# A linear-attention and two-MLP kernel: scores in column tiles of 32 keys, and column-tiled work in sessions

## The chip, the cores and the metric

One core of one Trainium2 chip. The metric is the time of one execution on the device, in microseconds (us); lower is better. A core has five engines: TensorE (PE; the profile has its weight loads as PEld), VectorE (DVE), ScalarE (ACT), GpSimd (POOL) and SyncE (SP), which here issues most of the DMAs. PE writes its results to PSUM, which has eight banks of 128 partitions by 512 floats; all other tiles lie in SBUF.

## The reference, cut to what matters

Three stages. A gated linear attention with a complex decay for 4 sequences of 768 steps, 8 heads of 48; a gated MLP without a nonlinearity; and a second MLP with 8 experts, of which each token takes one.

```python
for t in range(S):
    new_re = ar * S_re - ai * S_im
    new_im = ar * S_im + ai * S_re
    kv = np.einsum('bhd,bhe->bhde', k[:, :, t], v[:, :, t])
    S_re, S_im = (new_re + kv, new_im)
    y[:, :, t] = np.einsum('bhd,bhde->bhe', q[:, :, t], S_re)
x = y.transpose(0, 2, 1, 3).reshape(3072, 384)
x = (x @ w_a) * (x @ w_b) @ w_out
e = argmax(x @ w_gate);  out = gate * (relu(x @ w1[e]) @ w2[e])
```

## The kernel before, in words

**Blocks and chunks.** The 3072 tokens are cut into 12 blocks of 256 (`j` = 0 to 11; the text calls `j` = 3 the fourth), three blocks to a sequence, and each block into two chunks `c` of 128. The recurrence is worked out chunk by chunk in matrix form: within a chunk, scores of 128 keys by 128 queries under a causal mask; between chunks, a state `T`.

**Preprocessing** (`pre`, from L1139). From a, q and k it works out decays and phases on ACT, DVE and POOL, in tiles of which there is one each. Its last operations are the products of L1275 (k and q with the cosine and the sine, on POOL for most blocks) and twelve DMAs on SP (L1286, the turning loads) that set these products into `kT` and `qT`: 96 rows (real and imaginary part of 48) by head, chunk and token. The next block's preprocessing reuses the tiles that these DMAs read, and the next block's `kT` and `qT` those of this block.

**Attention** (`attn`, L1317 to 1443), for each chunk:

- `sc` (L1332 to 1335): scores, 4 heads to a PSUM bank, one product for each head over all of PE's 128 columns. An f32 product is two passes of PE, so four heads are eight passes.
- `mask` (L1337): DVE reads the bank, multiplies by the causal mask (-1 or 0) and writes `sm`.
- `kn` and `kept` (L1341, L1346): PE transposes `kT`, four heads at a time, and ACT copies the result to SBUF.
- `y` (L1351 to 1374): the output, in column tiles of 32: four products stand side by side on PE's 32-column strips. Each adds `sm` times v and `qT` times the state.
- `kv` (L1390 to 1394): the state's update, in three column tiles of 32; `sum_` and `fade` (L1396, L1405) apply it on DVE.
- `xH`, `xL` (L1381, L1387): y in two parts, which the MLP reads.

v of a chunk (L1109) lies in one of three buffers, with 64 floats to a head, of which 48 are loaded.

**The first MLP** (`planned_moe`, L1074), one block later: for each of 12 slices of the hidden width, `up` (18 products of 256 columns, L957), a gate on ACT, DVE and POOL (L974 to 991), and `down` (6 products of 392 columns, L1000). Block j - 1's MLP runs beside block j's attention and block j + 1's preprocessing.

**The order.** Every engine executes its instructions in the order in which the program lists them. Up to the last block's MLP that order comes from a planner (`Plan`, from L343). Each operation is given to it with an engine, a duration, what it reads and writes, and a due time `at`; it plays through the schedule and lets each engine take, of what is ready, the operation that is due first. `TIMES` (L47) shifts the due times of kinds of operations; the kinds numbered 4 are all blocks from the fifth on. Due times of successive blocks lie `SLOT` = 48.9 apart. The score banks are a ring of three (`P = Plan({"sc": 3})`, L834): scores, transposes, `kv` and the router's count take them in turn. Loads on SP wait in its queue, in the planner's order, until their buffer is free.

**The start.** POOL writes constants (L482 to 505, L1102) before its first preprocessing product (L1201).

**The end.** After the plan the last block's MLP and the experts run in an order of their own (from L1513).

## Time and profile before

| | us |
|---|---|
| median of 3 runs | 912.55 |
| lowest, highest run | 911.75, 915.97 |
| the profiled execution, its own time | 914.04 |
| its span, first to last instruction | 912.2 |
| mean granted TensorE clock in it | 0.992 |

The profile is of one execution. A span is the time from the first to the last instruction; the execution's own time has a little more around it. A product's duration in the timeline runs from its start to its modelled end, and products overlap; so the cost of a product on PE is read from the start of one to the start of the next. `x8` in a row counts the passes merged into it. "Idle before" is the time that the engine stood still ahead of an instruction, with what ended it in brackets.

### The profile page before, as it was taken

Reading aid. Unit: us, or ns where it says so; the run is one execution under the profiler, and the core shown is the slowest. Engines: PE = TensorE matmul, PEld = TensorE weight load, DVE = VectorE, ACT = ScalarE, POOL = GpSimd, SP = SyncE. Lnnn points to the kernel's source line nnn. Section 1 sums busy time; section 2 is a strip of 40 time slices with the busy share of each in tenths; the row PEclk is TensorE's granted clock in tenths of the full one; section 3 lists DMA queues with packets and bytes.
Section 4 is the critical chain, followed back from the end, with each engine's and each line's share of the span. In section 5 each row is a group of like instructions: output and inputs, shape, how many; then the busy total and the mean of one; then the engine's idle time right before and its main releaser. Section 6 shows DMA issues by size and latency. Waiting matters only on the chain.

```text
span 912.2 us, 20675 instructions
## 1 busy us (share of the span) xinstructions
PE 850.9 (93%) x8188; PEld 816.7 (90%) x8188; DVE 557.2 (61%) x1217; ACT 477.2 (52%) x887; POOL 352.5 (39%) x338
## 2 busy tenths in 40 slices
PE   0399999999999999999999999999995999999995
PEld 0387899999999999999999999999995999999995
DVE  6999997683838475666757593445731545455540
ACT  6487887574656474655655552224521534344430
POOL 2341441414454545363544444204163343444311
PEclk9999999999999999999999999999997999999998
DMA  9999964433242452627274524123341544454511
GB/s 254 276 279 236 244 142 124 103 90 100 69 96 81 109 170 65 200 60 217 63 208 69 167 59 145 36 88 122 105 153 35 160 133 138 147 161 129 164 51 25
DMA packets 134379, 120.17 MB, mean 132 GB/s; under 512 B 37284, under 2 KB 128820, under 8 KB 134271
## 3 DMA queue, kind: packets, MB, share of 16 engines
q1 hardware_dynamic: 121151, 100.51, 39.3%
q0 software_dynamic: 11392, 17.43, 8.3%
q8 instruction: 67, 1.10, 0.5%
q10 hardware_dynamic: 1728, 0.79, 0.4%
q14 instruction: 41, 0.34, 0.2%
HBM read 82.42 MB, written 10.56 MB: 102 GB/s over the span
## 4 chain that ended last, share of the span: by engine, by line
PE 72%; issue 13%; DMA 5%; POOL 5%; DVE 3%; SPq 1%; ACT 0%; POOLq 0%; DVEq 0%; ACTq 0%
PE ab_p L957 31%; PE o L1000 16%; PE h_p L771 4%; PE sc_p L1335 4%; PE y_p L1374 4%; PE o L803 4%; PE ab_p L965 3%; POOL gt L732 2%; POOL out_dram L814 2%; PE o L971 2%; PE kv_p L1394 2%; DMA out_dram<-ye,ids 1%; PE kn_p L1344 1%; DMA v<-in_v_dram 1%; DMA ids<-idtab 1%
## 5 line engine op out<-in xcount | busy, mean ns | idle before, releaser
L957 PE MATMUL ab_p<-xH,wL 128*128 128x256 f32 x792 | 220.9, 279 | 0.0
L957 PEld LDWEIGHTS ab_p<-xH,wL 128*128 128x128 f32 x792 | 148.8, 188 | 0.0
L991 POOL TENSOR_TENSOR gL<-g,gH 128x256 fp32r<-128x256 f32 x96 | 80.3, 838 | 171.4 <-ACT gH L987 166.9
L980 ACT COPY g<-ab_p 128x256 f32<-128x256 f32 x132 | 48.8, 370 | 133.6 <-PE ab_p L957 124.3
L983 DVE TENSOR_TENSOR g<-g,ab_p 128x256 f32<-128x256 f32 (+1 forms) x148 | 60.7, 410 | 90.3 <-ACT g L980 87.0
L957 PE MATMUL ab_p<-xH,waH 128*128 128x256 f32 x396 | 113.7, 287 | 0.0
L957 PE MATMUL ab_p<-xL,waH 128*128 128x256 f32 x396 | 111.1, 281 | 0.0
L957 PE MATMUL ab_p<-xH,wbH 128*128 128x256 f32 x396 | 110.6, 279 | 0.0
L957 PE MATMUL ab_p<-xL,wbH 128*128 128x256 f32 x396 | 110.4, 279 | 0.0
L1000 PE MATMUL o<-woH,gH 128*128 128x392 f32 x264 | 96.4, 365 | 0.0
L1000 PE MATMUL o<-wL,gH 128*128 128x392 f32 x264 | 90.3, 342 | 0.0
L1000 PE MATMUL o<-woH,gL 128*128 128x392 f32 x264 | 90.2, 342 | 0.0
L771 PE MATMUL h_p<-sH,w1H 128*128 128x256 f32 (+5 forms) x240 | 78.2, 326 | 11.2 <-issue 10.2
L803 PE MATMUL o<-w2H,h 128*128 128x384 f32 (+3 forms) x312 | 86.2, 340 | 0.0
L771 PE MATMUL h_p<-sL,w1H 128*128 128x256 f32 (+5 forms) x240 | 77.4, 323 | 0.0
L771 PE MATMUL h_p<-sH,w1L 128*128 128x256 f32 (+5 forms) x240 | 77.4, 322 | 0.0
L987 ACT ACTIVATE gH<-g 128x256 fp32r<-128x256 f32 x132 | 54.5, 413 | 40.3 <-DVE g L983 36.7
L957 PEld LDWEIGHTS ab_p<-xH,waH 128*128 128x128 f32 x396 | 74.5, 188 | 0.9 <-issue 0.2
L957 PEld LDWEIGHTS ab_p<-xL,waH 128*128 128x128 f32 x396 | 74.6, 188 | 0.4
L957 PEld LDWEIGHTS ab_p<-xL,wbH 128*128 128x128 f32 x396 | 74.5, 188 | 0.0
L957 PEld LDWEIGHTS ab_p<-xH,wbH 128*128 128x128 f32 x396 | 74.4, 188 | 0.0
L814 POOL DMA_INDIRECT out_dram<-ye,ids x29 | 30.2, 1040 | 92.9 <-ACT ye L813 84.2
(210 smaller groups left out, 2162.8 us busy)
## 6 DMA issues: line engine op xcount, KB each, us to landing
raw<-in_moe_w_dram SPq DMA_DIRECT2D x64, 384.0 KB
q<-in_q_dram SPq DMA_DIRECT2D x24, 192.0 KB
v<-in_v_dram SPq DMA_DIRECT2D x24, 192.0 KB
raw<-in_moe_w_a_dram SPq DMA_DIRECT2D x12, 384.0 KB
raw<-in_moe_w_b_dram SPq DMA_DIRECT2D x12, 384.0 KB
raw<-in_moe_w_out_dram SPq DMA_DIRECT2D x12, 384.0 KB
wL<-a POOLq DMA_DIRECT2D x24, 192.0 KB
x2d<-x SPq DMA_DIRECT2D x24, 192.0 KB
```

Source lines behind the costliest of these rows:

```text
L771: nc.tensor.matmul(out=t, lhsT=lh[:, o:o + 128], rhs=rh[:, kk], start=n == 0, stop=n == 8)
L803: nc.tensor.matmul(out=G["o", c], lhsT=lh, rhs=rh, start=f == 0 and n == 0, stop=f == NH - 1 and n == len(ops) - 1)
L814: d = nc.gpsimd.indirect_dma_start(out, bass.IndirectOffsetOnAxis(ap=ids[0:r, c:c + 1], axis=0), y[0:r], None, bounds_check=NT - 1, oob_is ...
L957: nc.tensor.matmul(out=t[:, i], lhsT=lh[:, kk * 128:(kk + 1) * 128], rhs=rh[:, kk], start=n == 0, stop=n == 8)
L965: nc.tensor.matmul(out=t[:, i], lhsT=A32[nm, f][:, kk * 128:(kk + 1) * 128], rhs=xT["F", 0][:, kk, cs[0]:cs[0] + len(cs)].rearrange("p c t ...
L980: nc.scalar.copy(out=G["g", j, f], in_=G["ab", j, f][:, 0])
L983: nc.vector.tensor_tensor(out=G["g", j, f], in0=G["g", j, f], in1=G["ab", j, f][:, 1], op=ALU.mult)
L987: nc.scalar.activation(out=G["H", j, f], in_=G["g", j, f], func=ACTF.Copy)
L991: eng.tensor_tensor(out=G["L", j, f], in0=G["g", j, f], in1=G["H", j, f].bitcast(F32), op=ALU.subtract)
L1000: nc.tensor.matmul(out=G["o", j, c], lhsT=lh[:, c * C:(c + 1) * C], rhs=rh, start=f == first and n == 0, stop=f == last and n == 2)
L1335: nc.tensor.matmul(out=S["p", hg][:, h], lhsT=pq["k", j][:, hg * 4 + h, c, :], rhs=pq["q", j][:, hg * 4 + h, c, 0:C], start=True, stop=True)
L1374: nc.tensor.matmul(out=t[q4 * 32:q4 * 32 + 32, kk], lhsT=a, rhs=b, start=f0, stop=f1)
```

## The change

From the fourth block on (`SWAP = 3`) a group of four heads' scores is computed in strips of 32 keys, each with the queries from its own first key on: `out=t[a:a + 32, r, b:C]`. Head `r` of a group puts strip `b` into partitions `(b + 32 r) % 128`, so that the four heads' products of one strip stand in four different column tiles. The keys of head `r` are thereby turned by 32 r partitions. The mask has four parts, one for each turn, and v is loaded three more times, turned in the same way (`vrot`; six DMAs on SP for each chunk, each of two heads). The parts of a bank that no strip writes are zeroed once: two of the three score banks are kept for scores for good (`emptied`, `kept_banks`), and the third serves transposes, `kv` and the router's count.

The PE work of a chunk is put to the planner in larger pieces: the scores of both groups of the first chunk; y and `kv` of the first chunk with the scores of the second; y and `kv` of the second chunk. The DVE and ACT operations stand between them as before. The tables of due times change for blocks from the fifth on. POOL writes the larger mask and the pads of `vrot` at the start. After the plan the score banks are given back and taken again as three.

```diff
+STRIP = 32
+SWAP, KEPT = 3, 2
...
-    ('pre', 4, 0, 0): (39.6, 1),
     ('pre', 4, 0, 1): (-35.1, 1),
-    ('pre', 4, 0, 3): (-31.5, 1),
+    ('pre', 4, 0, 3): (-111.2, 1),
...
-    ('attn', 4, 'PE'): (4.8735, 1),
+    ('attn', 4, 'PE'): (-8.1265, 1),
-    ('gate', 4): (-41.3, 1),
-    ('down', 4): (-9.1, 1),
+    ('gate', 4): (-105.6, 1),
+    ('down', 4): (-8.6, 1),
+    ('v', 4): (-66.3, 1),
+    ('loads', 4): (-16.5, 1),
+    ('pre', 4, 0, 2): (17.2, 1),
+    ('pre', 4, 0, 4): (48.5, 1),
...
+        p_sc = sctx.enter_context(tc.tile_pool(name="p_sc", bufs=1, space=bass.MemoryType.PSUM))
+        scores, phase, turns = [], [0], [0, 0]
+
+        def bank(shape, name):
+            if phase[0] == 2:
+                return p_sc.tile(shape, F32, tag="sc", name=name)
+            n = turns[phase[0]]
+            turns[phase[0]] += 1
+            return p_sc.tile(shape, F32, tag=f"s{n % 3}" if phase[0] == 0 else f"s{(turns[0] + n % (3 - KEPT)) % 3}", name=name)
...
-        causal = const.tile([128, 128], F32, name="causal")
-        nc.gpsimd.memset(causal, -1.0)
-        nc.gpsimd.affine_select(out=causal, in_=causal, pattern=[[1, 128]], compare_op=ALU.is_ge, fill=0.0, base=0, channel_multiplier=-1)
+        masks = ab.tile([128, 4, C], BF16, name="masks")
+        nc.gpsimd.memset(masks, -1.0)
+        causal = masks[:, 0]
+        nc.gpsimd.affine_select(out=causal, in_=causal, pattern=[[1, C]], compare_op=ALU.is_ge, fill=0.0, base=0, channel_multiplier=-1)
...
-        P = Plan({"sc": 3})
+        P = Plan({"sc": 3, "s1": 3 - KEPT})
...
+        vrot = [ab.tile([128, 3, 2, HP], F32, name=f"vr{i}") for i in range(3)]
         for t in vpad + tpad:
             nc.gpsimd.memset(t[:, :, D:HP], 0.0)
+        for t in vrot:
+            nc.gpsimd.memset(t[:, 0::2, :, 0:HP - D], 0.0)
+            nc.gpsimd.memset(t[:, 1, :, D:HP], 0.0)
+        for r in range(1, 4):
+            n = STRIP * (1 + (r == 2))
+            for a in range(0, C, n):
+                nc.gpsimd.affine_select(out=masks[a:a + n, r], in_=masks[a:a + n, r], pattern=[[1, C]], compare_op=ALU.is_ge, fill=0.0, base=-((a - r * STRIP) % C), channel_multiplier=-1)
+
+        def emptied(i):
+            scores.append(bank([128, 4, C], "scores"))
+            nc.vector.memset(scores[i], 0.0)
+
+        def kept_banks():
+            phase[0] = 1
...
+            def turned(r, x):
+                def f():
+                    t, n = vrot[(2 * j + c) % 3], r * STRIP
+                    a, b = ((0, n), (n, C))[x]
+                    o, p0 = (HP - D) * (r % 2), (2 * j + c) * C + (a - n) % C
+                    nc.sync.dma_start(out=t[a:b, r - 1, :, o:o + D], in_=v[p0:p0 + b - a, :].rearrange("p (x r d) -> p x r d", r=4, d=D)[:, :, r])
+                return f
+
+            if j >= SWAP:
+                for r in range(1, 4):
+                    for x in range(2):
+                        P.add("SP", 0.5, turned(r, x), kind=("v", min(j, 4)), w=[("vr", (2 * j + c) % 3, r, x)], at=at, early=at, size=12 * (r, 4 - r)[x])
...
+        def ring(j):
+            return "sc" if j < SWAP else "s1"
...
+            if j == SWAP:
+                for i in range(KEPT):
+                    P.add("DVE", 0.55, lambda i=i: emptied(i), r=["kept"], w=["banks", ("scores", i)], at=t0 - 10)
+                P.add("SP", 0.0, kept_banks, w=["banks", "kept"], at=t0 - 10)
...
                 def sc(hg, c=c, S=S):
-                    S["p", hg] = p_sc.tile([128, 4, C], F32, tag="sc", name="sc_p")
-                    for h in range(4):
-                        nc.tensor.matmul(out=S["p", hg][:, h], lhsT=pq["k", j][:, hg * 4 + h, c, :], rhs=pq["q", j][:, hg * 4 + h, c, 0:C], start=True, stop=True)
+                    t = S["p", hg] = bank([128, 4, C], "sc_p") if j < SWAP else scores[hg % KEPT]
+                    if j < SWAP:
+                        for h in range(4):
+                            nc.tensor.matmul(out=t[:, h], lhsT=pq["k", j][:, hg * 4 + h, c, :], rhs=pq["q", j][:, hg * 4 + h, c, 0:C], start=True, stop=True)
+                        return
+                    for b in range(0, C, STRIP):
+                        for r in range(4):
+                            a = (b + r * STRIP) % C
+                            nc.tensor.matmul(out=t[a:a + STRIP, r, b:C], lhsT=pq["k", j][:, hg * 4 + r, c, b:b + STRIP], rhs=pq["q", j][:, hg * 4 + r, c, b:C], start=True, stop=True)
...
-                    nc.vector.tensor_tensor(out=S["s", hg], in0=S["p", hg], in1=causal.unsqueeze(1).to_broadcast([128, 4, C]), op=ALU.mult)
+                    nc.vector.tensor_tensor(out=S["s", hg], in0=S["p", hg], in1=masks if j >= SWAP else causal.unsqueeze(1).to_broadcast([128, 4, C]), op=ALU.mult)
...
-                                ops.append((ld["v", j, c].rearrange("p h d -> p (h d)")[:, o:o + 32], S["s", h // 4][:, h % 4]))
+                                if h % 4 and j >= SWAP:
+                                    vt = vrot[(2 * j + c) % 3].rearrange("p r x d -> p (r x d)")
+                                    vo = o - h * HP + (h % 2) * (HP - D) + ((h % 4 - 1) * 2 + h // 4) * HP
+                                else:
+                                    vt, vo = ld["v", j, c].rearrange("p h d -> p (h d)"), o
+                                ops.append((vt[:, vo:vo + 32], S["s", h // 4][:, h % 4]))
...
+                if j >= SWAP:
+                    P_ = [("scores", i) for i in range(KEPT)]
+
+                    def both(c=c, sc=sc):
+                        for hg in range(2):
+                            sc(hg)
+
+                    if c == 0:
+                        add("PE", 1.54, both, qk + [("kT", 0), ("qT", 0)], P_)
+                    else:
+                        rest, after, r_, w_ = pending.pop()
+
+                        def joined(rest=rest, both=both):
+                            for f in rest:
+                                f()
+                            both()
+
+                        add("PE", 4.05 - (0.9 if first_b else 0), joined, r_ + qk + [("kT", 1), ("qT", 1)], w_ + P_, take=ring(j))
+                        for a, kw in after:
+                            add(*a, **kw)
+                        if j + 1 < NB:
+                            todo.append(("v", 0, None, (), (), {}))
                     for hg in range(2):
-                        add("PE", 0.33, at_(kn, hg), qk + [("kT", c)], [("kn_p", j, c, hg)], take="sc")
-                        add("ACT", on("ACT", 384, True), at_(kept, hg), [("kn_p", j, c, hg)], [("kn", 0), ("kn", 1)] if hg == 0 else [("kn", 1)], give=True)
-                add("PE", 1.0 if first else 1.9, y, [("sm", 0), ("sm", 1), v_, ("qT", c)] + ([] if first else [T_]) + qk, ["y"])
-                if j:
-                    add("ACT", on("ACT", 384, True), xH, ["y"], [("xH", j % 2)] + ([("x", j % 2)] if c == 0 else []) + ([("x", 0, 0), ("x", 0, 1)] if j == 2 and c == 0 else []))
-                    add("DVE", on("DVE", 384), xL, ["y", ("xH", j % 2)], [("x", j % 2)], alone=False)
+                        add("DVE", on("DVE", 512), at_(mask, hg), [("scores", hg % KEPT)], [("sm", hg)], alone=False)
+                    if not last:
+                        for hg in range(2):
+                            add("PE", 0.3, at_(kn, hg), qk + [("kT", c), "kept"], [("kn_p", j, c, hg)], take=ring(j))
+                            add("ACT", on("ACT", 384, True), at_(kept, hg), [("kn_p", j, c, hg), "banks"], [("kn", 0), ("kn", 1)] if hg == 0 else [("kn", 1)], give=True)
+                    r_ = [("sm", 0), ("sm", 1), v_, ("qT", c)] + vr_ + ([] if first else [T_]) + qk + ([] if last else [("kn", 0), ("kn", 1), "kept"])
+                    w_ = ["y"] + ([] if last else [("kv_p", j, c)])
+                    after = []
+                    if not last:
+                    after += [(("ACT", on("ACT", 384, True), xH, ["y"], [("xH", j % 2)] + ([("x", j % 2)] if c == 0 else []) + ([("x", 0, 0), ("x", 0, 1)] if j == 2 and c == 0 else [])), {}),
...
+                    rest = [y] + ([] if last else [kv])
+                    if c == 0:
+                        pending.append((rest, after, r_, w_))
+                    else:
+                        add("PE", 2.7 if not last else 1.95, lambda rest=rest: [f() for f in rest], r_, w_, **({} if last else dict(take=ring(j))))
+                        for a, kw in after:
+                            add(*a, **kw)
...
-            t = P.add("PE", 0.2, count, r=["oh", "acc"], w=["rk_p"], at=at + 2, take="sc")
-            P.add("DVE", 1.1, place, r=["rk_p", "oh"], w=["acc", "posu"], at=at + 2, give=t)
+            t = P.add("PE", 0.2, count, r=["oh", "acc", "kept"], w=["rk_p"], at=at + 2, take=ring(j))
+            P.add("DVE", 1.1, place, r=["rk_p", "oh", "banks"], w=["acc", "posu"], at=at + 2, give=t)
...
+        phase[0] = 2
+        sctx.close()
+        p_sc = sctx.enter_context(tc.tile_pool(name="p_sc1", bufs=3, space=bass.MemoryType.PSUM))
+        P2[0] = p_sc
```

Left out above: the same calls of `bank` in place of a tile of `p_sc` in the other helpers, reads of `"banks"` and `"kept"` that order the change of the banks, and a renaming of the first block's MLP buffers.

## Rows read from the trace of the kernel before

**Rows 1.** The page, part 1: busy us, share, instructions.

```profile
PE 850.9 (93%) x8188; PEld 816.7 (90%) x8188; DVE 557.2 (61%) x1217; ACT 477.2 (52%) x887; POOL 352.5 (39%) x338
```

**Rows 2.** Stretches: length, PE, PEld, DVE, ACT, POOL, clock, DMA share, GB/s.

```profile
250.00:300.00 50.00, 50.00 (x553) 48.80 (x555) 29.44 (x63) 30.97 (x56) 25.19 (x22) 1.00 0.33 81
...
400.00:450.00 50.00, 49.82 (x567) 48.15 (x566) 31.53 (x71) 27.34 (x50) 22.58 (x22) 1.00 0.41 116
```

**Rows 3.** The chain in order of time: start us, us, work.

```profile
357.47 1.90 PE y_p L1374 x64
...
370.09 2.12 PE ab_p L957 x18
...
603.25 1.90 PE y_p L1374 x64
```

**Rows 4.** Timeline of PE: start us, us; scores of four heads.

```profile
282.94 1.06 PE L1335 MATMUL sc_p<-qT,kT 96*128 96x128 f32 x8
283.75 0.42 PE L1000 MATMUL o<-woH,gH 128*128 128x392 f32 x1
284.01 0.34 PE L1000 MATMUL o<-wL,gH 128*128 128x392 f32 x1
284.19 0.34 PE L1000 MATMUL o<-woH,gL 128*128 128x392 f32 x1
```

**Rows 5.** Timeline of PE, y of a chunk between products of the MLP.

```profile
294.10 0.28 PE L957 MATMUL ab_p<-xH,wL 128*128 128x256 f32 x1
294.31 0.43 PE L1374 MATMUL y_p<-sm,v 128*32 128x128 f32 x8
...
295.87 0.40 PE L1374 MATMUL y_p<-qT,T 96*32 96x128 f32 x8
296.20 0.45 PE L1000 MATMUL o<-woH,gH 128*128 128x392 f32 x1
296.49 0.34 PE L1000 MATMUL o<-wL,gH 128*128 128x392 f32 x1
```

**Rows 6.** Timeline of PE, y and the state update back to back.

```profile
201.24 1.08 PE L1374 MATMUL y_p<-sm,v 128*32 128x128 f32 x32
202.14 0.86 PE L1394 MATMUL kv_p<-v,kn 128*32 128x48 f32 x48
202.93 0.45 PE L1000 MATMUL o<-woH,gH 128*128 128x392 f32 x1
```

**Rows 7.** Line 912, eight-column products: duration ns min/median/max.

```profile
L912 PE MATMUL wg_p<-wg,wt x288: 172/176/222, 29.2 to 112.6; 128*32 128x8 f32 x144
```

**Rows 8.** Timeline of PE, the same 24 passes in one run.

```profile
83.58 0.38 PE L912 MATMUL wg_p<-wg,wt 128*32 128x8 f32 x24
```

**Rows 9.** Groups by line: busy us, mean ns, idle before.

```profile
L1339 DVE TENSOR_TENSOR sm<-sc_p,causal 128x512 f32<-128x512 f32 x48 | 32.8, 686 | 18.0 <-PE sc_p L1335 17.6
...
L1349 ACT COPY kn<-kn_p 128x384 f32<-128x384 f32 x40 | 18.8, 476 | 9.3 <-PE kn_p L1344 6.4 <-PE wt_p L902 2.5
```

**Rows 10.** Timeline of POOL at the start.

```profile
1.47 0.28 POOL L483 TENSOR_SCALAR_AFFINE_SELECT causal<-causal 128x128 f32<-128x128 f32 x1
...
2.55 0.48 POOL L1102 MEMSET v<- 128x128 f32 x3
...
4.97 0.83 POOL L1201 TENSOR_TENSOR Bt<-im 128x384 f32<-128x384 f32 x1 [1.65 <-DMA im<-in_a_im_dram]
```

**Rows 11.** Timeline of DVE at the start.

```profile
13.21 0.36 DVE L883 TENSOR_SCALAR a<-raw 128x384 uint32<-128x384 uint32 x1 [1.42 <-DMA raw<-in_moe_w_a_dram]
```

**Rows 12.** Timeline of SP's queue at the end of a block.

```profile
410.86 0.60 SPq L1109 DMA_DIRECT2D v<-in_v_dram  x1
411.55 2.63 SPq L1286 DMA_DIRECT2D kT<-Bt  x3
```

**Rows 13.** Timeline of POOL, last product of a preprocessing pass.

```profile
406.02 1.74 POOL L1275 TENSOR_TENSOR q<-q,X 128x768 f32<-128x768 f32 x1
...
455.79 1.76 POOL L1275 TENSOR_TENSOR q<-q,X 128x768 f32<-128x768 f32 x1
```

More of the change, by code (lines that the diff above doesn't have):

```diff
@@ L67 @@
     'less': (-1.8, 0.8),
-    'high': (-0, 0.89),
+    'high': (0, 0.89),
     ('pre', 2, 0, 0): (-70.8, 1),
@@ L526, in counted @@
         def counted():
-            sorting["t"] = p_sc.tile([128, NE], F32, tag="sc", name="so_p")
+            sorting["t"] = bank([128, NE], "so_p")
             nc.tensor.matmul(out=sorting["t"], lhsT=ones16, rhs=acc, start=True, stop=True)
@@ L635, in count @@
                     base = eoff
-                t = p_sc.tile([128, 2, NE], F32, tag="sc", name="rk_p")
+                t = bank([128, 2, NE], "rk_p")
                 for c in range(2):
@@ L898, in turned @@
             def turned():
-                K["t"] = p_sc.tile([128, 3, C], F32, tag="sc", name="wt_p")
+                K["t"] = bank([128, 3, C], "wt_p")
                 for kk in range(3):
@@ L908, in folded @@
             def folded():
-                K["t"] = p_sc.tile([128, NE], F32, tag="sc", name="wg_p")
+                K["t"] = bank([128, NE], "wg_p")
                 for kk in range(3):
@@ L1390, in kv @@
                 def kv(c=c, S=S):
-                    t = S["kv"] = p_sc.tile([96, H, D], F32, tag="sc", name="kv_p")
+                    t = S["kv"] = bank([96, H, D], "kv_p")
                     for h in range(H):
@@ L1411, in at_ @@
                     return lambda: f(*a)
-                for hg in range(2):
-                    add("PE", 0.9, at_(sc, hg), qk + [("kT", c), ("qT", c)], [("sc_p", j, c, hg)], take="sc")
-                    add("DVE", on("DVE", 512), at_(mask, hg), [("sc_p", j, c, hg)], [("sm", hg)], give=True, alone=False)
-                if not last:
-                    for hg in range(2):
-                        add("PE", 0.33, at_(kn, hg), qk + [("kT", c)], [("kn_p", j, c, hg)], take="sc")
-                        add("ACT", on("ACT", 384, True), at_(kept, hg), [("kn_p", j, c, hg)], [("kn", 0), ("kn", 1)] if hg == 0 else [("kn", 1)], give=True)
@@ L1426, in attn @@
[L1426 to L1430 removed]
+                if j >= SWAP:
[16 more added lines that the diff above has]
+                            todo.append(("v", 0, None, (), (), {}))
+                    for hg in range(2):
+                        add("DVE", on("DVE", 512), at_(mask, hg), [("scores", hg % KEPT)], [("sm", hg)], alone=False)
[7 more added lines that the diff above has]
+                    if not last:
+                        after += [(("DVE", on("DVE", 384), sum_, [("kv_p", j, c), T_, "banks"] + qk, [To_]), dict(give=True, alone=False)), (("DVE", 0.01 if first else on("DVE", 384), fade, [To_] + qk, [To_]), {})]
+                    after += [(("ACT", on("ACT", 384, True), xH, ["y"], [("xH", j % 2)] + ([("x", j % 2)] if c == 0 else []) + ([("x", 0, 0), ("x", 0, 1)] if j == 2 and c == 0 else [])), {}),
+                              (("DVE", on("DVE", 384), xL, ["y", ("xH", j % 2)], [("x", j % 2)]), dict(alone=False))]
+                    rest = [y] + ([] if last else [kv])
[5 more added lines that the diff above has]
+                            add(*a, **kw)
+                else:
+                    for hg in range(2):
+                        if j < SWAP:
+                            add("PE", 0.9, at_(sc, hg), qk + [("kT", c), ("qT", c)], [("sc_p", j, c, hg)], take="sc")
+                            add("DVE", on("DVE", 512), at_(mask, hg), [("sc_p", j, c, hg), "banks"], [("sm", hg)], give=True, alone=False)
+                        else:
+                            p_ = ("scores", hg % KEPT)
+                            add("PE", 0.64, at_(sc, hg), qk + [("kT", c), ("qT", c)], [p_])
+                            add("DVE", on("DVE", 512), at_(mask, hg), [p_], [("sm", hg)], alone=False)
+                    if not last:
+                        for hg in range(2):
+                            add("PE", 0.33, at_(kn, hg), qk + [("kT", c), "kept"], [("kn_p", j, c, hg)], take=ring(j))
+                            add("ACT", on("ACT", 384, True), at_(kept, hg), [("kn_p", j, c, hg), "banks"], [("kn", 0), ("kn", 1)] if hg == 0 else [("kn", 1)], give=True)
+                    add("PE", 1.0 if first else 1.9, y, [("sm", 0), ("sm", 1), v_, ("qT", c)] + vr_ + ([] if first else [T_]) + qk, ["y"])
+                    if j:
+                        add("ACT", on("ACT", 384, True), xH, ["y"], [("xH", j % 2)] + ([("x", j % 2)] if c == 0 else []) + ([("x", 0, 0), ("x", 0, 1)] if j == 2 and c == 0 else []))
+                        add("DVE", on("DVE", 384), xL, ["y", ("xH", j % 2)], [("x", j % 2)], alone=False)
+                    else:
+                        add("ACT", on("ACT", 384, True), x32, ["y"], [("x", 0, c)])
+                    if not last:
+                        add("PE", 0.82, kv, [("kn", 0), ("kn", 1), v_, "kept"], [("kv_p", j, c)], take=ring(j))
+                        add("DVE", on("DVE", 384), sum_, [("kv_p", j, c), T_, "banks"] + qk, [To_], give=True, alone=False)
+                        add("DVE", 0.01 if first else on("DVE", 384), fade, [To_] + qk, [To_])
@@ L1431, in attn @@
+                if c == 0 and j < SWAP and j + 1 < NB:
                     todo.append(("v", 0, None, (), (), {}))
```

30 lines of the change are left out of this document (14 added, 16 removed).

## The prediction

> **What bounds the kernel now.** I read the page first, then the stretches, the chain in order of time, and last the single instructions. TensorE is busy for 93% of the span [rows 1]. In the stretch where the planner lays attention beside the first MLP, it is busy for all of 50 us or nearly, at the full granted clock, while VectorE, ScalarE and GpSimd have 29 to 32, 27 to 31 and 23 to 25 us of work and the DMA engines a share of 0.33 to 0.41 [rows 2]. The chain agrees: it runs through PE's products there, and the y product of a block's second chunk comes back 603.25 - 357.47 = 245.78 us later after five blocks, so a block takes 49.16 us [rows 3]. The reader should see that PE hardly waits in this stage: a microsecond less of PE work per block is a microsecond less of time, for as long as nothing else needs the whole block. Nine of the twelve blocks are changed.
>
> **The scores, from the rows.** Four heads' scores are eight passes. They start at 282.94 and the next product at 283.75; that product's successor comes after 0.26 us where 0.18 is usual [rows 4]. One group so costs 0.81 + 0.08 = 0.89 us. After the change a group is 16 products, 32 passes, in strips of 128, 96, 64 and 32 queries, four column tiles side by side. The y product is of that shape already (96 rows, 32 columns, 128 moving): seven of its sets of eight passes take 295.87 - 294.31 = 1.56 us, 0.223 each [rows 5], so four tiles do run side by side, 28 ns a pass. If a strip's time goes with its columns, a group takes 0.223 x (1 + 0.75 + 0.5 + 0.25) = 0.56 us. If it doesn't, 4 x 0.223 = 0.89: nothing won. Two rows speak for columns. The state update has 48 columns in three tiles; its 48 passes take 0.79 us up to the next product [rows 6], of which 0.11 is the step out of the session (below), so 14 ns a pass, and 28 x 48/128 x 4/3 is 14 as well. And the eight-column products of line 912 run 24 passes in 0.38 us, less one duration of 0.176 about 0.20, so 9 ns a pass [rows 7, 8]; only the 32-query strip (7 ns by its columns) meets that floor. I take 0.57 us, near the low end because both rows lie there, and keep 0.89 for the range. A group wins 0.32 us, the 36 groups of nine blocks 11.5 us.
>
> A rule speaks against this. The Trainium skill's page "TensorE: Matmul & The Clock Gate", in its section on the 56 ns against 53.3 ns, says that matmuls never start closer than about 25 ns however few columns they have. By it 32 passes take an estimated 0.80 us, a group wins 0.09, and the 36 groups 3.2 us. The 14 and 9 ns of [rows 6 to 8] differ from it: starts in different column tiles stand closer here.
>
> **The sessions, from the rows.** Between column-tiled and whole-array work PE loses time. Into y: 294.31 - 294.10 = 0.21 us where an up product's pitch is 2.12/18 = 0.12, so 0.09. Out of it: the last set ends at 295.87 + 0.22 = 296.09, the next product starts at 296.20 and its successor 0.29 us later where 0.18 is usual, so 0.22 [rows 3, 5]. Together 0.31 us. Where the state update follows y directly, nothing lies between (32 passes in 0.90 us, four sets of 0.223) [rows 6]. In the trace the blocks from the fourth on have four sessions (y and kv of two chunks, each by itself); three where a sequence ends, which has no second kv, and in the fourth block, where [rows 6] join one pair. Afterwards it is three everywhere: scores; y, kv and the next scores; y and kv. Five blocks win 0.31, 1.6 us in all. **Sum on PE: 11.5 + 1.6 = 13.1 us, 1.46 a block.**
>
> **What is given back.** *One bank.* Two of the three score banks are kept, so the key transposes (two groups a chunk), kv and the router's count take turns in one. A turn costs ScalarE's copy of 0.48 us [rows 9] and two hand-overs. It is hidden by MLP products of 2.12 us [rows 3] set between; uncovered, it would be some 0.8 us for each of five turns a block. Zero here. *The new wait.* y now waits for both key copies too, because kv is in its session; behind it on PE's queue stand the next up and down products, and ScalarE's gate copies wait for those. Its cover is the same 2.12 us products. *Masks* read another tile, at 512 elements as before (0.69 us [rows 9]), off PE's path: zero, with VectorE's 18 free us in 50 as cover; without it 0.69 a group. *Changed due times and weights* only reorder: zero, and at best they win back PE's gaps, 0.2 us in 50 [rows 2], 1.2 us in all.
>
> *The start.* GpSimd gets ten mask selects (0.28 us) and six memsets (0.48/3 = 0.16) ahead of its first product, 3.8 us, where it now idles 1.65 us for a load [rows 10]. The product slips by 2.1 us; VectorE idles 1.42 us for another load before 13.21 [rows 11], which takes up most. Bounds 0 and 2.1; I take 0.5, near the low end, since 1.42 of the 2.1 are idle anyway. *Changing the banks* at the fourth block needs all three drained and two VectorE memsets, each at most a mask's 0.69: bounds 0 and 2, taken 0.5 for the MLP products beside it.
>
> *SP's queue.* Each of 18 chunks adds six loads of rotated v, 144 KB, small beside a DMA share of 0.41 [rows 2]. Their issue is another matter. At a block's end the v load frees itself with kv and goes out at 410.86, in 0.60 us, just ahead of the twelve turning loads that start at 411.55 [rows 12]; six more pieces there delay those by 3.6 us. Behind them wait the next preprocessing pass, which needs the tiles they read, and the next scores. A pass, from the v load at 410.86 to its last product at 455.79 + 1.76 = 457.55 [rows 12, 13], takes 46.7 us; the pass before ended at 407.76, 3.8 us ahead of its turning loads. With the pieces it is 50.3, against a block of 49.16 - 1.46 = 47.70. So 2.6 us a block are missing unless the pass closes up. Bounds: 0 (the pieces issued behind the turning loads, or the pass closed up) and 2.6 us for each of eight steps, 21 us. The three engines of the pass have 18 to 27 us free in 50 [rows 2], so I take 0.4 us a block, 3.2 us, near the low end.
>
> **Sum:** -13.1 + 0.5 + 0.5 + 3.2 = -8.9 us. The durations are from the profiled execution of 914.04 us (span 912.2, 1.8 around it), which would become 905.1; it stands 1.5 above the median of 912.55, from which I forecast 903.7.
>
> **Rivals.** *A: strips get no shorter with fewer columns.* Then only the sessions win: -1.6 + 1.0, so 912.0 us. [rows 6 to 8] are against it; chance 0.05. By the page's 25 ns it would be -4.8 + 1.0, 908.8 us, and that is within this chance.
>
> *C: the preprocessing loop holds the block where it was.* If it closes up only to 49.16 us, PE's gain turns into waits before the scores and in the sessions: 1.46 x 8 = 11.7 us given back, 912.55 - 13.1 + 1.0 + 11.7 = 912.2. For it speaks that the loop is already 46.7 of 49.2 us; against it that its engines are half idle. Chance 0.12.
>
> *B, slower: the six pieces stand ahead of the turning loads and the pass doesn't close up.* Place: SP's queue at a block's end. Price 2.6 us a block, 21 in all; it decides from 1.5 a block. 912.55 - 13.1 + 1.0 + 21 = 921.5 us. For it: v is freed before the turning loads are and has gone first [rows 12]. Against it: the planner knows the queue and can set the pass closer. Chance 0.11.
>
> **How the numbers follow.** The forecast, with the pass closing up by most of what it must, has 0.72; its own range is 898 (all of 13.1, the gaps won back) to 908. Of this kernel 0.5%, 4.6 us, is about what a measurement can tell from no change. A and C lie within it, so the same has 0.17; B is slower with 0.11; faster has 0.72. The range, 898 to 913 us, takes in the forecast, A and C and leaves out B and a little below.
>
> **What would show it.** Right: a group of scores near 0.57 us in the timeline, no gap between y, kv and scores, three steps out of a session a block, y of the second chunk back after some 48.1 us, and PE still busy all of 50. Wrong by A: sets of eight passes that stay at 0.22 us for every strip. Wrong by C or B: idle time of PE before scores or y, released by kT or qT loads, the twelve turning loads issued after six v pieces, and a pass that ends just ahead of the next. The start would show in GpSimd's first product after 4.97 us.

## The result: slower, and the profile after

The changed kernel took 922.85 us in the median of four runs (921.53 to 929.56), the kernel before 913.59 us in four runs on the same chip: a ratio of 1.0105, 95% interval 1.0067 to 1.0142. The forecast was 903.7 us, faster. The profiled execution took 923.34 us with a span of 921.6.

TensorE lost work, as it was meant to: on the page after, busy time is 845.4 us where [rows 1] have 850.9.

```profile
PE 845.4 (92%) x9052; PEld 812.8 (88%) x9052; DVE 568.0 (62%) x1219; ACT 475.6 (52%) x887; POOL 352.5 (38%) x354
```

But it now waits where it had been full. These are the two stretches of [rows 2] and the one behind them, of the kernel after (length, PE, PEld, DVE, ACT, POOL, clock, DMA share, GB/s):

```profile
250.00:300.00 50.00, 48.53 (x664) 47.12 (x663) 28.52 (x64) 27.92 (x51) 23.67 (x21) 1.00 0.37 93
400.00:450.00 50.00, 47.54 (x648) 46.79 (x647) 34.67 (x66) 26.99 (x49) 20.99 (x19) 0.97 0.46 126
...
450.00:500.00 50.00, 47.53 (x570) 46.62 (x569) 32.19 (x70) 27.71 (x49) 22.58 (x20) 0.93 0.51 134
```

Two things are to be seen: 2.5 us of 50 in which PE does nothing, and a clock below 1. What the waits are for, the waits of PE from 373.09 to 574.81 us say (line, what it waited for, us in total, times, longest):

```profile
PE scores L1396 <- DMA kT<-k: 2.5, 1, 2.5
PE scores L1396 <- DMA qT<-q: 2.5, 1, 2.5
PE scores L1396 <- DMA ck<-in_moe_w_a_dram: 2.0, 1, 2.0
PE scores L1396 <- DMA k<-in_k_dram: 1.9, 1, 1.9
```

Four blocks, four waits, 8.9 us, all at the scores that open a block; the kernel before has 0.2 us in its own four blocks. The scores wait for the turning loads. (Two rows name other loads. In both, the load named went out within 0.6 us of the block's last turning load, at 369.56 and 523.36; they are read as the same wait.) The timeline of SP's queue ahead of one of these waits answers [rows 12]:

```profile
406.60 0.57 SPq L1142 DMA_DIRECT2D v<-in_v_dram  x1
407.22 4.40 SPq L1150 DMA_DIRECT2D vr<-in_v_dram  x6
411.72 1.88 SPq L1332 DMA_DIRECT2D kT<-Bt  x3
413.70 1.83 SPq L1332 DMA_DIRECT2D kT<-k  x3
415.63 1.84 SPq L1332 DMA_DIRECT2D qT<-A  x3
417.56 2.54 SPq L1332 DMA_DIRECT2D qT<-q  x2
420.21 0.54 SPq L1172 DMA_DIRECT2D k<-in_k_dram  x1
420.80 0.55 SPq L1332 DMA_DIRECT2D qT<-q  x1
```

SP is free at 406.60, and the first turning load goes out 5.12 us later: six pieces of vr at 0.73 us each stand between. GpSimd has the product for this load ready at 405.54 + 1.83 = 407.37, so some 4.3 us are the pieces' (timeline of POOL):

```profile
405.54 1.83 POOL L1321 TENSOR_TENSOR Bt<-k,X 128x768 f32<-128x768 f32 x1
```

The pieces serve a chunk one and a half blocks ahead (there are three tiles vr, and two chunks in a block); the turning loads serve the scores that PE is about to begin. PE begins them at 424.91, and not only late (timeline of PE, start us, us):

```profile
424.91 2.33 PE L1396 MATMUL scores<-qT,kT 96*32 96x128 f32 x64 [2.46 <-DMA qT<-q]
427.17 0.58 PE L972 MATMUL ab_p<-xH,waH 128*128 128x256 f32 x1
```

The 64 passes take 2.26 us to the next product; undisturbed, 15 us on, they take 1.23. The windows behind the waits show why:

```profile
425.00:430.00 5.00, 5.00 (x83) 4.94 (x84) 5.00 (x8) 3.42 (x6) 2.56 (x3) 0.66 0.88 281
473.00:478.00 5.00, 4.75 (x75) 4.72 (x76) 5.00 (x11) 3.58 (x6) 2.15 (x2) 0.50 0.98 293
```

0.50 of 2.4 GHz is the lower of the clock's two levels, 1.2 GHz, and 0.66 is a stretch partly at either. TensorE stood idle for some 2 us, the clock fell, and the work behind the wait ran at half speed for a while. This is so at three of the four waits; behind the first, of 1.94 us at 374.67, the clock stayed at 1.00.

The strips and sessions themselves are as forecast. One chunk's y, its kv and the next scores, in the timeline of PE:

```profile
439.78 0.40 PE L1440 MATMUL y_p<-qT,T 96*32 96x128 f32 x8
440.00 0.82 PE L1460 MATMUL kv_p<-v,kn 128*32 128x48 f32 x45
...
440.68 1.30 PE L1396 MATMUL scores<-qT,kT 96*32 96x128 f32 x63
441.91 0.45 PE L1018 MATMUL o<-woH,gH 128*128 128x392 f32 x1
442.20 0.34 PE L1018 MATMUL o<-wL,gH 128*128 128x392 f32 x1
```

There is no gap in the session. Both groups of scores take 441.91 - 440.68 = 1.23 us, 0.62 each (forecast 0.57; less the 0.11 us ahead of the next product that the forecast counts with the step out, it is 0.56), and the rest of the step out is the 0.29 us to the second product, as in [rows 5]. The 64 passes start 19 ns apart on average. The Trainium skill's page "TensorE: Matmul & The Clock Gate", in its section on the 56 ns against 53.3 ns, would have them never closer than about 25 ns; here, across four column tiles, the trace differs.

**Where the 9 us came from, by blocks.** ScalarE copies each MLP block's first output out of PSUM (x<-o); the start of that copy is a mark for each of the twelve blocks. The third, sixth, tenth and last of the kernel after, from ScalarE's timeline:

```profile
219.97 0.48 ACT L1026 COPY x<-o 128x384 f32<-128x384 f32 x1 [1.95 <-PE o L1018]
...
373.09 0.47 ACT L1026 COPY x<-o 128x384 f32<-128x384 f32 x1
...
574.81 0.46 ACT L1026 COPY x<-o 128x384 f32<-128x384 f32 x1
...
655.63 0.48 ACT L1026 COPY x<-o 128x384 f32<-128x384 f32 x1 [1.25 <-PE o L1018]
```

The same marks of all kernels, in us ("period" is a quarter of the time from sixth to tenth):

| kernel | 3rd | 6th | 10th | last | period | ratio to before, 95% interval |
|---|---|---|---|---|---|---|
| before | 214.75 | 365.07 | 560.80 | 645.41 | 48.93 | 1 |
| after | 219.97 | 373.09 | 574.81 | 655.63 | 50.43 | 1.0105 (1.0067 to 1.0142) |
| e1 pieces behind | 222.58 | 369.85 | 558.94 | 639.71 | 47.27 | 0.9897 (0.9879 to 0.9915) |
| e2 no pieces | 221.43 | 368.87 | 558.38 | 639.27 | 47.38 | 0.9916 (0.9888 to 0.9945) |
| e3 before with pieces | 215.83 | 370.93 | 571.15 | 655.73 | 50.05 | 1.0122 (1.0105 to 1.0139) |
| e4 late set-up | 218.08 | 369.98 | 570.19 | 650.99 | 50.05 | 1.0068 (1.0047 to 1.0090) |
| e5 pieces unseen | 217.54 | 365.46 | 554.88 | 636.12 | 47.36 | 0.9895 (0.9875 to 0.9914) |
| e6 unseen, late set-up | 215.90 | 363.59 | 554.15 | 635.30 | 47.64 | 0.9892 (0.9874 to 0.9911) |
| e7 strips alone | 216.17 | 371.46 | 566.86 | 649.24 | 48.85 | 1.0047 (1.0030 to 1.0064) |
| e8 sessions alone | 216.85 | 371.75 | 565.00 | 647.19 | 48.31 | 1.0016 (1.0004 to 1.0028) |
| e9 after again | 220.07 | 374.33 | 570.55 | 651.47 | 49.05 | 1.0081 (1.0054 to 1.0107) |
| e10 before with set-up | 214.12 | 363.93 | 558.97 | 643.48 | 48.76 | 1.0008 (0.9999 to 1.0017) |
| e11 old due times | 216.18 | 362.45 | 557.52 | 641.72 | 48.77 | 0.9938 (0.9922 to 0.9954) |
| e12 old due times, behind | 215.38 | 362.78 | 554.42 | 641.93 | 47.91 | 0.9966 (0.9947 to 0.9986) |

The change stands 5.2 us behind at the third mark, when only the first changed block has run; it loses 2.8 us to the sixth and 6.0 to the tenth, where PE was to win 1.46 a block; and wins 3.8 over the last two blocks. Times in us don't carry from the first runs to e1 to e11, which ran on three chips: what follows the last mark took 912.2 - 645.41 = 266.8 us there and 895.8 - 643.48 = 252.3 in e10, the kernel before but for its set-up. So the totals in the expectations, given for 913 us, are read as ratios. The marks carry better, but not exactly: e10's period is 48.76 us where the first profile of before has 48.93. e12 ran on a fourth, in this like the first (909.2 - 641.93 = 267.3). Two of e12's twelve runs, 924.06 and 1213.07 us at a lower clock, belong to a slower state and are not in its ratio.

### The profile page after: what moved, and what is told of

The parts are those of the page before. It is cut to its first block, busy times and chain, and to the rows that moved or that the text cites. A ratio compares the mean times of both kernels' runs of the same rounds, so it can differ in the third digit from the quotient of the medians.

```text
span 921.6 us, 22556 instructions
## 1 busy us (share of the span) xinstructions
PE 845.4 (92%) x9052; PEld 812.8 (88%) x9052; DVE 568.0 (62%) x1219; ACT 475.6 (52%) x887; POOL 352.5 (38%) x354
## 3 DMA queue, kind: packets, MB, share of 16 engines
q8 instruction: 75, 1.23, 0.6%
## 4 chain that ended last, share of the span: by engine, by line
PE 57%; issue 13%; DMA 7%; POOL 7%; SPq 6%; DVE 5%; ACT 1%; another core or an unknown queue 1%; POOLq 0%; ACTq 0%; DVEq 0%
PE ab_p L972 21%; PE o L1018 12%; PE y_p L1440 4%; SPq L1332 4%; PE h_p L786 4%; PE o L818 4%; PE ab_p L980 3%; PE scores L1396 3%; POOL out_dram L829 2%; POOL gt L747 2%; DMA qT<-q 2%; PE o L986 1%; PE kv_p L1460 1%; PE kn_p L1405 1%
## 5 line engine op out<-in xcount | busy, mean ns | idle before, releaser
L1001 DVE TENSOR_TENSOR g<-g,ab_p 128x256 f32<-128x256 f32 x132 | 54.7, 414 | 131.2 <-ACT g L998 129.0
L797 DVE SCALAR_TENSOR_TENSOR h<-h_p,h 128x384 fp32r<-128x384 f32 (+1 forms) x48 | 26.6, 555 | 66.6 <-ACT h L795 58.5
```

The costliest lines, as they stand in the source:

```text
L1001: nc.vector.tensor_tensor(out=G["g", j, f], in0=G["g", j, f], in1=G["ab", j, f][:, 1], op=ALU.mult)
```

## The experiments

In each kernel only what is named is changed; the diffs show the main lines, and "..." stands for lines left out. Theory 1 puts the loss in the place of the pieces on SP, theory 2 in the sessions and banks, theory 3 in the start.

**e1: the pieces behind the turning loads.** The planner's result is kept and only the pieces (P.pieces) are moved: a group with turning loads, or loads of q, k, re or im, among the next two SP tasks is issued behind the block's load of im (P.last).

```
-        for x, n, _ in out:
-            ops[n]["f"]()
+        for n in self.behind([n for _, n, _ in out]):
+            ops[n]["f"]()
```

> The changed kernel with the same order on every engine, only that a group of pieces of vr that stands ahead of turning loads or of the loads of q, k, re, im is issued behind them (behind the load of im). Theory 1 (the pieces ahead of the turning loads on SP make the loss: they push the turning loads back by 4.4 us where SP is released at 406.6 us, and the third block's loads of q and k by some 19 us at 95 us): period of blocks 4 to 9 from 50.4 to 47.5-48.5 us, close of the third block's MLP (219.97) back to 216 or so, total 903-909 us. Theory 2 (the sessions and the two banks left to the other users make the loss, the pieces are covered): within 2 us of 922.9. Theory 3 (the start on POOL makes the first 5 us): close of the third block's MLP stays at 219-220 us whatever the steady blocks do, total 908-914 us.

889.77 us against 898.52, ratio 0.9897: 913 us would become 904. The period fell from 50.43 to 47.27 us, 1.66 below before. Moving DMA issues on one queue, with nothing else changed, turns the loss into the gain that was forecast. Theory 1 holds for the blocks from the sixth mark on. It missed the early part: the third mark stayed at 222.58, since TensorE's planned order, made with the pieces ahead, was kept.

**e2: the pieces not loaded.**

```
                 def f():
                     t, n = vrot[(2 * j + c) % 3], r * STRIP
+                    if 2 * j + c < 2 * SWAP + 3 and (r, x) == (1, 0):
+                        nc.gpsimd.memset(t, 0.0)
+                    return
```

> The changed kernel with the same order, but the turned pieces of v are never loaded (the tile vr is cleared once, so y reads zeros there). Theory 1: as the kernel with the pieces behind the turning loads, or up to 3 us below it, since the pieces' descriptors leave the DMA engines too: 900-908 us. Theory 2: 920-923 us. If this kernel is more than 4 us below the one with the pieces behind, the pieces cost by their traffic and not by their place.

Ratio 0.9916, period 47.38: no better than e1, though its page counts 134,386 DMA packets where e1's has 149,939. So the pieces' traffic costs nothing that shows; their place does.

**e3: the pieces alone, in the kernel before.**

```
                 nc.sync.dma_start(out=t[:, :, 0:D], in_=v[...])
+                if j >= 3:
+                    for r in range(1, 4):
+                        for x in range(2):
+                            ...
+                            nc.sync.dma_start(out=t[a:b, r - 1, :, o:o + D], in_=v[p0:p0 + b - a, :]...)
```

> The kernel before, with six DMAs of the same shapes (into a tile that nobody reads) issued behind each load of v from the fourth block on, and nothing else changed: no strips, no sessions. Theory 1: the turning loads come 4 us later in every second group, block period from 48.9 to 50.5-52 us, total 922-935 us. Theory 2: 913-916 us, as before.

Ratio 1.0122, as much as the whole change. The period is 50.05, somewhat under the 50.5 expected. The queue looks as in the change, the turning loads 5.2 us behind the v load (timeline of SP, e3):

```profile
417.33 0.57 SPq L1110 DMA_DIRECT2D v<-in_v_dram  x1
417.96 4.50 SPq L1117 DMA_DIRECT2D vr<-in_v_dram  x6
422.55 1.87 SPq L1294 DMA_DIRECT2D kT<-Bt  x3
```

From the sixth to the tenth mark PE does little more than before and waits 3.9 us. The rows are the windows of before and of e3:

```profile
365.07:560.80 195.73, 195.55 (x2175) 190.34 (x2174) 128.44 (x288) 109.74 (x198) 92.56 (x80) 1.00 0.48 129
```

```profile
370.93:571.15 200.22, 196.28 (x2175) 189.95 (x2174) 128.68 (x288) 108.33 (x199) 91.76 (x80) 1.00 0.51 133
```

Here the clock stays at 1.00: the longest single wait is 1.7 us. The two long waits of PE are not at the scores, but both lead back to a load behind six pieces (timelines of SP, DVE, PE and ACT, e3):

```profile
460.17 0.52 SPq L567 DMA_DIRECT2D ck<-in_moe_w_a_dram  x1
463.70 1.01 DVE L570 TENSOR_REDUCE span<-ck 128x1 f32<-128x384 f32 x2 [4.25 <-DMA ck<-in_moe_w_a_dram]
465.69 0.42 PE L1382 MATMUL y_p<-sm,v 128*32 128x128 f32 x8 [1.73 <-DVE sm L1347]
...
525.01 0.84 ACT L1211 ACTIVATE Bt<-im 128x768 f32<-128x768 f32 x1 [4.67 <-DMA kT<-Bt]
526.62 0.39 PE L957 MATMUL ab_p<-xH,waH 128*128 128x256 f32 x1 [1.72 <-DVE g L983]
```

In the first, VectorE waits for a load of ck that went out right behind the pieces of 454.16, and the masks stand behind it. In the second, ScalarE's preprocessing waits for a turning load (521.16, behind the pieces of 516.94), and the gate that PE needs stands behind that. So the same place in the queue costs by other ways in another order of tasks. With e1 to e3, theory 2 is out as the cause of the loss.

**e4: the set-up late, in the changed kernel.**

```
-        for r in range(1, 4):
-            ...
-                nc.gpsimd.affine_select(out=masks[a:a + n, r], ...)
+        def turned_masks():
+            ...
```

(called, with the memsets of vr, where the first piece stands.)

> The changed kernel with the masks of the turned heads and the pads of vr made on POOL where the first piece of vr stands, instead of ahead of POOL's first product. Theory 3: the first product starts at 5.0 us as before instead of 7.5, and the close of the third block's MLP comes down by 4-5 us, total 917-919 us. Theory 1: the start gains 0.4 us at DVE's first cast and at most 1.5 us at the first matmuls, the third block's loads stay late, total 921-923 us.

GpSimd's first product came back to 5.18 us, and the third mark by 1.9 us, not the 4 to 5 of theory 3. Ratio 1.0068, and 1.0081 for the change itself on a like chip (e9): the intervals overlap, so what it is worth in the change isn't resolved. Its period, 50.05, lies by those of the change (50.43, and 49.05 in e9) and not by e1's.

**e5 and e6: the pieces unseen by the planner, and behind; e6 with the late set-up too.**

```
-  P.add("SP", 0.5, turned(r, x), kind=("v", min(j, 4)), ..., at=at, early=at, size=...)
+  P.pieces.add(P.add("SP", 0.0, turned(r, x), ..., at=at, early=at))
```

> As the kernel with the pieces behind the turning loads, and the planner now gives the pieces no time and no due time of their own, so that TensorE's order up to the third block is again that of the kernel before. Theory 1a (the loss ahead of the fourth block comes from the early due times of the pieces, which in the plan push back the third block's loads of q and k, and with them TensorE's order): closes of the first three blocks' MLPs within 2 us of before (121.2, 171.8, 214.8) instead of 125.8, 179.8, 222.6; last close 633-636 instead of 639.7; ratio to before 0.982-0.986. Theory 1b (the loss there comes from the start on POOL or from the masks, not from the plan): third close stays at 220-222, ratio 0.988-0.991.

> The kernel of the line above with the masks of the turned heads and the pads of vr made late on POOL. Both theories: the start costs 0.4 us at DVE's first cast and some 1.5 us at the first matmuls, so 0.5-1.5 us below the kernel without this step if nothing else waits in the first 100 us; 0 if the first blocks have slack.

Ratios 0.9895 and 0.9892. The third mark came from 222.58 to 217.54 and 215.90, the last from 639.71 to 636.12 and 635.30: in the profiled executions the early due times of the pieces make most of the early loss (e5 is still 2.8 us behind before, where 2 were expected). The medians, though, are those of e1, and the expected 0.982 to 0.986 was missed. One reason is likely, but not shown: e1's profiled execution took 893.91 us at a mean clock of 0.993, its other three 888.8 to 890.7 at 0.994 to 0.996. Its profile has a fall of the clock behind a wait of 2.6 us at the third block's scores; the others need not have had it. Only one execution of each run has a profile, so what the early order costs in the others stays open. In e5 the turning loads follow the v load, and the pieces the load of im (timeline of SP):

```profile
398.62 0.57 SPq L1164 DMA_DIRECT2D v<-in_v_dram  x1
400.22 1.88 SPq L1356 DMA_DIRECT2D kT<-Bt  x3
...
406.29 1.85 SPq L1356 DMA_DIRECT2D qT<-q  x3
...
415.67 0.37 SPq L1194 DMA_DIRECT2D im<-in_a_im_dram  x1
416.08 3.83 SPq L1172 DMA_DIRECT2D vr<-in_v_dram  x6
```

These windows, from the sixth to the tenth mark of after, of e9 (the change again, below) and of e5, split the loss:

```profile
373.09:574.81 201.72, 193.22 (x2550) 189.91 (x2554) 140.09 (x287) 106.74 (x195) 88.89 (x79) 0.97 0.47 127
```

```profile
374.33:570.55 196.22, 188.73 (x2550) 185.45 (x2554) 135.35 (x287) 106.91 (x194) 88.91 (x79) 0.99 0.48 131
```

```profile
365.46:554.88 189.42, 188.84 (x2562) 185.14 (x2564) 132.93 (x288) 107.33 (x197) 90.27 (x80) 1.00 0.49 134
```

Idle: 201.72 - 193.22 = 8.50 us in after against 0.58 in e5. The same matmuls: 193.22 us against 188.84. Of the 12.3 us between them 7.9 are waiting and 4.4 are slower work at the lower clock. In e9, on a chip like e5's, the difference is 6.8 us: idle 7.49, and busy 188.73, as in e5. So the waiting is there each time, 1.7 to 2.0 us a block; the slower work shows in after and not in e9, where the clock fell behind one of the four waits.

**e7 and e8: the strips alone, the sessions alone.** e7 is e5 with the tasks of the other branch (scores of each group, kn, y, kv by themselves); e8 is the change with scores of full width (the planner is given 0.26 us more for them), plain v in y, and no pieces or turned masks.

```
e7  -                if j >= SWAP:
    +                if False:
                         P_ = [("scores", i) for i in range(KEPT)]
e8  -                    if j < SWAP:
    +                    if True:
                             for h in range(4):
```

> The strips with the pieces unseen and behind, but without the sessions: scores of each group, kn, y, kv as tasks of their own again. By the sum of the prediction the joined session is worth 0.31 us a block (the switch between y and kv and between kv and scores): last close 1.5-3 us later than with sessions, ratio 0.2-0.3 per cent higher. If the sessions cost (a wait for kn and for the two banks inside one long task), the last close comes earlier than with them.

> The sessions with scores of full width: no strips, no pieces, no turned masks. By the sum of the prediction: 1.6 us below before (0.31 us a block of five), period of blocks 4 to 9 at 48.6 us, ratio 0.997-1.000. If the two banks that are left to kn, kv and the counts cost a wait, ratio 1.002-1.01.

These were the surprise: the strips alone made the kernel slower, 1.0047, and so did the sessions alone, 1.0016. The periods show that the price of a session was about right and its count what matters. Take 0.31 us a session and 4 x 0.32 us for the strips of a block. Of the four blocks between the marks one ends a sequence and has three sessions in before, so before has 3.75 on average. e5 has three: -1.28 - 0.23 = -1.51 us, measured 47.36 - 48.93 = -1.57. e8 has two: -0.54, measured -0.62. e7 has four more than before (each of four score groups is a session of its own now): -1.28 + 1.24 = -0.04, measured -0.08. Against e10's 48.76 the three are -1.40, -0.45 and 0.09, and e6, with the strips and sessions of e5, has 47.64; so the fit is good to some 0.2 us and no closer. One such group in e7's timeline of PE, with the step into it and out of it:

```profile
371.08 0.34 PE L1040 MATMUL o<-woH,gL 128*128 128x392 f32 x1
371.35 0.76 PE L1420 MATMUL scores<-qT,kT 96*32 96x128 f32 x32
372.05 0.39 PE L994 MATMUL ab_p<-xH,waH 128*128 128x256 f32 x1
372.27 0.28 PE L994 MATMUL ab_p<-xL,waH 128*128 128x256 f32 x1
372.40 0.28 PE L994 MATMUL ab_p<-xH,wL 128*128 128x256 f32 x1
```

0.27 us into it where down products follow at 0.18, 0.70 in it, and 0.22 behind it where up products follow at 0.12. Both kernels lose 5 us between the third and sixth mark instead (155.3 and 154.9 us against 150.3), where e8 has one wait of 3.4 us for GpSimd's gL, with a clock of 0.66 in the 5 us behind it. The due times were set for another mix of tasks; that they do it is not shown. e7's expectation, 0.2 to 0.3 per cent above the kernel with sessions, was missed by far (1.0047 against 0.9895): it counted one session where e7 has five more than e5, and not this loss.

**e9 and e10: the change again; the set-up alone, in the kernel before.** e10 adds the masks and memsets of the change ahead of GpSimd's first product, with every engine's order as before.

```
+        vrot = [ab.tile([128, 3, 2, HP], F32, name=f"vr{i}") for i in range(3)]
+        ...
+                nc.gpsimd.affine_select(out=masks[a:a + n, r], ...)
```

> The changed kernel itself, unedited, on the chip and beside the runs of before that the other kernels here are compared with. Ratio 1.007-1.014 as in the result; last close of an MLP block at 653-657 us in the profile.

> The kernel before with nothing added but the set-up on POOL (masks of the turned heads in bfloat16, pads of vr) ahead of POOL's first product; order on every engine otherwise that of before. If the start is a small part of the first 5 us: DVE's first cast 0.4 us later, the first three closes 1-2 us later than 121.2, 171.8, 214.8, ratio 1.000-1.002. If it makes the whole of it: closes 4-5 us later, ratio 1.004-1.006.

The change again: 1.0081, slower as before; its last mark at 651.47 instead of 655.63 and below the expected 653, with a period of 49.05 and four waits as before, 7.8 us, but a mean clock of 0.99 in the four blocks where the first profile has 0.97. The waits recur; how far the clock falls behind them varies. e10: 1.0008 (0.9999 to 1.0017), 0.7 us, although GpSimd's first product starts at 7.54 us as in the change:

```profile
4.06 3.39 POOL L1111 TENSOR_SCALAR_AFFINE_SELECT masks<-masks 32x128 bf16<-32x128 bf16 x10
7.54 0.83 POOL L1210 TENSOR_TENSOR Bt<-im 128x384 f32<-128x384 f32 x1
```

Its first three marks (121.00, 171.20, 214.12) are no later than those of before, where 1 to 2 us were expected. Theory 3 is out as the cause of the loss. VectorE's first cast is 0.41 us later (13.62 in e10 for 13.21 in [rows 11]).

**e11 and e12: the due times of before.** e11 is the change with the table TIMES of before, e12 is e6 with it.

```
-    ('gate', 4): (-105.6, 1),
...
-    ('v', 4): (-66.3, 1),
-    ('loads', 4): (-16.5, 1),
+    ('gate', 4): (-41.3, 1),
```

> The changed kernel with the due times of the kernel before (no times of their own for the loads of v of the later blocks, so the pieces' due times lie later); strips, sessions, banks and pieces as in the change. In the order that results TensorE's first three blocks stand as in before, but in each later block two to six of the pieces still stand ahead of or between the turning loads. Theory 1: between the two: period of blocks 4 to 9 48.0-50.0 us, ratio 0.992-1.006. If the due times themselves were the cause and not the pieces' place: period 47.4 us, ratio 0.988-0.990.

> The kernel with the pieces unseen by the planner, behind the turning loads, and the set-up late, now also with the due times of the kernel before. If what is left of the loss after the third block (150.3 us from the third to the sixth close before, 147.7 us with the change's due times, where the prediction's terms give 145.9 us) comes from the changed due times, ratio 0.984-0.988; if the changed due times are worth what they were made for, 0.990-0.995; if they matter only for the pieces, 0.988-0.990.

e11: 0.9938, between the two, as theory 1 had it: with the old due times the planner lets some of the pieces slip between the turning loads by itself. So the due times that came with the change are what put all of the pieces first. e12: 0.9966, worse than e6 and outside all three ranges that were expected; its last mark is 6.6 us later (641.93 for 635.30). By that the new due times are worth 0.7 per cent for the rest of the tasks, though the two ran on different chips. The fastest versions are those with the change's due times and the pieces issued behind the turning loads (e1, e5 and e6, not told apart).

## Why the prediction was wrong, point by point

- **The scores: right.** 0.56 to 0.62 us a group for 0.57 forecast; over whole blocks the strips' 1.28 us fit e5 and e7 to some 0.2 us. Rival A is out.
- **The sessions: right,** in that 0.31 us each fits e5, e7 and e8 as closely. PE's sum of 1.46 us a block came in as 1.29 to 1.66 in the kernels without the wait (e6 and e1 at the ends).
- **One bank, the new wait, the masks: right at zero.** None of them is among the waits of PE in after's four blocks. The one bank is not free in every order: in e12 a transpose waits 2.40 us for ScalarE's copy out of it.

```profile
260.81 0.62 PE L1430 MATMUL kn_p<-ident,kT 96*128 96x96 f32 x4 [2.40 <-ACT kn L1435]
```

- **The start: right.** Taken 0.5 us, measured 0.7 (-0.1 to 1.5) by e10. GpSimd's product slipped 2.57 us (2.1 forecast) and VectorE's cast 0.41 (0.7 left over). In the change's own order the late set-up brings the third mark 1.6 us (e6 against e5) to 2.0 us (e4 against e9) forward, but the last only 0.5 to 0.8.
- **SP's queue: the step that failed.** "The three engines of the pass have 18 to 27 us free in 50 [rows 2], so I take 0.4 us a block, 3.2 us, near the low end." The place and the mechanism were named (six pieces behind the v load, ahead of the turning loads), and the price of 2.6 us a block too. Measured against e5, a block costs 50.43 - 47.36 = 3.07 us in after, 2.70 in e4 and 1.69 in e9, with 1.7 to 2.0 us of waiting in each; to the last mark it is 655.63 - 636.12 = 19.5 us, and 15.4 in e9, where 3.2 were taken. The free time of the engines was the wrong row to decide by. The turning loads wait for nobody's free time: they stand in a queue of which the head waits for v's tile, and the scores of the same block wait for them. To have been right the step needed that wait, not a mean of busy shares.
- **What it left out.** The clock had no price: 1.1 of after's 3.07 us are work at the lower level behind the waits (in e9 nothing that shows). And "*Changed due times and weights* only reorder: zero" was wrong from the other side: the due times of the pieces put them first (e11), and ahead of the fourth block they sent the third block's loads of q and k out at 113.34 and 114.47 us instead of 96.13 and 95.30, behind twelve pieces.
- **Which rival.** B, with a chance of 0.11 and 921.5 us; measured 922.85. It fits in kind, and in size by luck: it has eight steps of 2.6 us. Of after's 19.5 us over e5, 2.4 lie ahead of the third mark, 5.2 between it and the sixth, 12.3 up to the tenth, and none in the last two blocks, which have no such wait and kept their gain. In e9 the period, 49.05, is nearer to C's 49.16.
- **Not settled.** From the third to the sixth mark e5 wins 2.4 us where three blocks should win over 4; 0.7 us of e5's stretch is idle time of PE (0.3 in before), the rest has no row. e12, made to ask whether the changed due times do it, takes 147.4 us there for e5's 147.9, but with its wait of 2.40 us in it, so that stays open.

## What to carry to other kernels

A new DMA costs by what it stands ahead of on its queue, first of all where the head of the queue already waits for a buffer. Look who waits for the next issues, and put transfers that are needed late behind those that are needed now. Where a wait of PE of about 2 us appears in a stage that was full, look at the granted clock behind it too: here the slower work added between nothing and 1.1 us a block. Between column-tiled and whole-array work count the changes as well as the passes: the strips alone won nothing, since each group paid for its own step in and out.

## What was not expected of the hardware

- The clock fell to its lower level behind waits of PE as short as 1.73 us (e11, at 230.12) and 1.88 us (after, at 147.78), and behind 1.99 to 2.85 us in after, e1, e4 and e9 (granted clock 0.50 or 0.66 in the 5 us behind). It stayed at 1.00 behind others of 1.85 us (e9), 1.94 (after), 1.97 (e4) and 3.16 (e2). So the length of a wait alone did not tell whether the clock fell.
- Ten mask selects on 32 or 64 partitions took 3.39 us, 0.34 each, where a select on all 128 took 0.28 [rows 10], in bfloat16 too (at 1.80 in after): fewer partitions were no cheaper.
- Passes of matmuls started 19 ns apart on average across four column tiles, over 64 passes of 32 to 128 columns.
